# Loads that name 4 as their outermost dimension become four loads of 32 rows, and two kinds of decay rows get a DRAM array each

## The chip, the cores and the metric

The kernel runs on one core of a Trainium2 chip. Its engines are TensorE (PE, matrix products), VectorE (DVE), ScalarE (ACT), GpSimd (POOL) and SyncE (SP), which here only issues transfers; sixteen DMA engines move the data. The metric is the time of one execution on the device in microseconds (us). Three runs of the kernel before gave 586.14, 586.71 and 587.26 us; the median is 586.71.

## The reference

Three stages follow one another on 3072 tokens (4 sequences of 768). The first is a linear attention with decay, for 8 heads of width 32 and a state of 16; in chunks, with a running sum `cum` of log(a):

```
L = exp(cum_i - cum_j), zero above the diagonal
M = (C B^T) * L
y = M x + (C state) * exp(cum)
state = exp(sum log a) * state + sum_j (B_j x_j) * exp(cum_last - cum_j)
```

The second normalises each token by its root mean square and applies a gated network, `silu(xn @ w_gate) * (xn @ w_val) @ w_out`, with 256 columns in and out and 1536 between. The third is `h = x @ w_in` (1024 columns), `h * softmax(h)`, a layer norm over the 1024 columns, and a product with `w_out` back to 256 columns.

## The kernel before

The 3072 tokens are 24 units of 128 tokens; four units make a block of 512 columns, and there are six blocks. Each unit passes through the attention (functions whose names begin with `at_`), then its block through the gated network (`g_` and `o_mm`), then each unit through the third stage (`m_`). The stages of neighbouring blocks are interleaved, so that PE always has products of one block while DVE and ACT prepare another. Matrix products are made of float32 values split in a high and a low part, three products for one.

No engine chooses its work at run time. A planner (`plan`) takes a list of operations, each with an engine, an estimated duration, a due time and what it comes after, and lays them out one by one; each engine then works through its own list in that order and waits in front of an operation until its inputs are there. For SP the planner counts 8 transfers in flight at most, and its estimate of a landing goes by the `kb` and `us` of the operation. The transfers of SP carry 8 semaphores in turn (`DMAHW0` to `DMAHW7`), so a transfer is issued when the one eight before it has landed.

For one attention unit SP loads five things. `xb` (L204) is x and B of the unit, 128 rows; DVE or POOL scale its B part by the decay (L220). `cd` (L199) is C, transposed, in which the 32 rows of `bcT[u]` go to four groups of 32 partitions; it is multiplied by `e1` (L239). `L` (L216) and `e1` (L210) are decay rows: early on, `c_store` (L958) writes for each of the 192 pairs of unit and head a row of 256 numbers into the DRAM array `crow`, the first 128 for `L` and the last 128 for `e1`. `L` is that part of 8 rows given to all 128 partitions, `e1` the other part of 8 rows, each given to 16 partitions. ACT takes exponents of `L` (L226). The fifth is `bc`: B and C of the unit. For the first 12 units these are two loads of 16 rows (L194); from unit 12 (`SPLIT`) on it is one load of 512 KB that gives the 32 rows of `bcT[u]` to four groups of 32 partitions (`ld_bc4`, L308), from which B and C in high and low parts are made (L313 to L334). PE makes C B^T of a unit into the PSUM tile `pcb` (tag `hc`), DVE multiplies it with `L` (L297, L300), and the third stage's `ph` (L471) needs the same PSUM banks, so it waits for these products.

In the third stage of 20 units the 128 x 1024 block is transposed by DVE in squares of 32 (L553, into `dt`), stored to DRAM (`scr`, L559), and loaded in four pieces with the squares in their places (`tt`, four loads of 32 partitions, L566). ACT and DVE split it in high and low parts (`uth` L571, `utl` L576) for PE's product `pf` (L600). Then the result goes out (L608).

In SP's list the loads of a coming attention unit stand between the store `scr` and the reload `tt` of the unit that is in the third stage.

Of the kernel before, what the change touches and what calls it, by code (L numbers as in the profile page):

```python
# [7 lines left out]
F32 = mybir.dt.float32  # L8
# [7 lines left out]
P = 128  # L16
NU = 24
NH = 8
# [32 lines left out]
def fused_kernel(ctx, tc, aT, xbt, bcT, wg, wv, wo1, rg, wi2, wo2, gl, consts, out):  # L51
    nc = tc.nc
    V, A, G, T, S = nc.vector, nc.scalar, nc.gpsimd, nc.tensor, nc.sync
# [5 lines left out]
    dp = ctx.enter_context(tc.tile_pool(name="dram", bufs=1, space=bass.MemoryType.DRAM))  # L59
# [25 lines left out]
    la = cp.tile([P, NU * NH], F32, name="la")  # L85
    cneg = cp.tile([P, NU * NH], F32, name="cneg")
    wdec = cp.tile([P, NU * NH], F32, name="wdec")
    crow = dp.tile([NU * NH, 2 * P], F32, name="crow")


    def wt(shape, nm):
# [58 lines left out]
    wm = {}  # L150
# [45 lines left out]
    def ld_cd(u):  # L196
        d = st.setdefault(u, {})
        d["cd"] = sp.tile([P, P], F32, name="cd")
        S.dma_start(d["cd"], bcT[u][:, 512:1024].rearrange("r (q i) -> q r i", q=4))  # L199

    def ld_xb(u):
        d = st.setdefault(u, {})
# [3 lines left out]
    def ld_e1(u):  # L206
        d = st.setdefault(u, {})
        d["e1"] = sp.tile([P, P], F32, name="e1")
        r = crow[u * 8:u * 8 + 8, P:2 * P]
        S.dma_start(d["e1"], r.unsqueeze(1).to_broadcast([8, 16, P]))  # L210

    def ld_L(u):
        d = st.setdefault(u, {})
        d["L"] = sp.tile([P, 8, P], F32, name="L")
        r = crow[u * 8:u * 8 + 8, 0:P]
        S.dma_start(d["L"], r.unsqueeze(0).to_broadcast([P, 8, P]))  # L216

    def at_bw(u, e):
        bw = st[u]["xb"][:, DM:].rearrange("p (h n) -> p h n", h=8)
# [56 lines left out]
    def cbt(u):  # L276
        return u < blk[0][1] and u % 2
# [27 lines left out]
    def ld_bc4(u):  # L305
        d = st.setdefault(u, {})
        d["bc"] = sp.tile([P, 8, P], F32, name="bc")
        S.dma_start(d["bc"], bcT[u].unsqueeze(0).to_broadcast([4, 32, 1024]))  # L308

    def at_hi(u):  # L310
        d = st[u]
# [370 lines left out]
    def op(name, e, us, due, fn, after=(), new=(), use=(), lock=False, kb=0):  # L682
        ops[name] = dict(name=name, e=e, us=us, due=due, fn=fn, after=list(after), new=list(new), use=list(use),
                         lock=lock, kb=kb)

    def alt(name, us, fn):
        ops[name]["alt"] = (us, fn)
# [30 lines left out]
    for i in range(26):  # L718
        t = wdue(i)
        kind, c = pieces[i][0]  # L720
        op(f"wl{i}", "SP", 0.45, EARLY[i] if i < len(EARLY) else t - 6, (w_load, i), after=[f"wl{i-1}"] if i else [], new=[("u", f"st{i}")], kb=512)
        for k in range(3):
            op(f"wc{i}.{k}", "DVE", 0.41 if k == 0 else 0.68, t, (w_conv, i, k),
               after=[f"wl{i}" if k == 0 else f"wc{i}.{k-1}"],
               new=[("wt", f"wt{i}")] if k == 0 else [], use=[f"st{i}", f"wt{i}"], lock=True)
        if kind == "p":
            op(f"wh{i}", "ACT", 0.7, t, (p_scale, i), after=[f"wc{i}.2", "glt"] + ([f"wh{i-1}"] if c else []), use=[f"wt{i}", "w2h", "w2l"],
               new=[("uth", "w2h"), ("utl", "w2l")] if c == 0 else [])
# [18 lines left out]
    for u in range(NU):  # L747
        b, k = unit_blk[u]
        n = blk[b][1]
        if b == 0:  # L750
            Y = Y0[0] + Y0[1] * k
        else:
            Y = start[b - 1] + (k + YPOS) * (start[b] - start[b - 1]) / n * YSPAN
        s0 = u % 6 == 0
        if u >= SPLIT:
            op(f"lbc{u}", "SP", 0.45, Y - 14, (ld_bc4, u), new=[("bc", f"bc{u}")], kb=1300)
            op(f"hi{u}", "ACT", 1.15, Y - 6, (at_hi, u), after=[f"lbc{u}"] + ([f"cb{u-1}"] if u > SPLIT else []),
               new=[("wt", f"bh{u}"), ("wt", f"ch{u}")], use=[f"bc{u}", f"bh{u}", f"ch{u}"])
            op(f"bl{u}", "DVE", 0.7, Y - 5, (at_blo, u, V), after=[f"hi{u}"], use=[f"bc{u}", f"bh{u}"], lock=True)
            alt(f"bl{u}", 1.3, (at_blo, u, G))  # L760
            op(f"cl{u}", "DVE", 0.72, Y - 5, (at_clo, u), after=[f"hi{u}"], use=[f"bc{u}", f"ch{u}"], lock=True)
            op(f"c0{u}", "ACT", 0.7, Y - 4, (at_c0, u), after=[f"cl{u}"], new=[("u", f"cb{u}")], use=[f"bc{u}", f"cb{u}"])
            op(f"c1{u}", "DVE", 0.45, Y - 4, (at_c1, u), after=[f"c0{u}"], use=[f"bc{u}", f"cb{u}"], lock=True)
            cbok = [f"bl{u}", f"c0{u}", f"c1{u}"]
        else:
            op(f"lbc{u}", "SP", 0.85, Y - 9, (ld_bc, u), new=[("bc", f"bc{u}")], kb=128)
            cbok = [f"lbc{u}"]
        op(f"lxb{u}", "SP", 0.45, Y - 7.5, (ld_xb, u), new=[("xb", f"xb{u}")], kb=192)
        op(f"lcd{u}", "SP", 0.45, Y - 7, (ld_cd, u), new=[("cd", f"cd{u}")], kb=128)
        op(f"bw{u}", "DVE", 0.3, Y - 1, (at_bw, u, V), after=[f"lxb{u}", "wd"], use=[f"xb{u}"], lock=True)  # L770
        alt(f"bw{u}", 0.42, (at_bw, u, G))
        if u < NPE:
            for g in range(2):
                tg = ("pg", "pv")[g]
                op(f"lpe{u}.{g}", "PE", 0.9, Y - 5, (at_lpe, u, g), new=[(tg, f"pl{u}.{g}")], use=[f"pl{u}.{g}"],
                   after=[f"lpe{u}.{g-1}"] if g else [])
                op(f"lx{u}.{g}", "ACT", 1.3, Y - 5, (at_lpx, u, g), after=[f"lpe{u}.{g}"] + ([f"lx{u}.{g-1}"] if g else []), use=[f"pl{u}.{g}", f"L{u}"],
                   new=[("L", f"L{u}")] if g == 0 else [])
                op(f"ls{u}.{g}", "POOL", 0.57, Y - 4, (at_lselh, u, g), after=[f"lx{u}.{g}"], use=[f"L{u}"], lock=True)
            if u == 0:  # L780
                op("e1p", "PE", 0.3 * NPE, Y - 3, (at_e1pe,), new=[("po0", "pe")], use=["pe"])
                op("e1x0", "ACT", 0.6, Y - 3, (at_e1x,), after=["e1p"], new=[("th", "e1")], use=["pe", "e1"])
            e1, e1x = "e1", "e1x0"
            Lok = [[f"ls{u}.0"], [f"ls{u}.1"]]
        else:
            op(f"le1{u}", "SP", 0.45, Y - 8, (ld_e1, u), after=["crow"], new=[("e1", f"e1{u}")], kb=64)
            op(f"lL{u}", "SP", 0.6, Y - 11, (ld_L, u), after=["crow"], new=[("L", f"L{u}")], kb=512)
            op(f"lx{u}.0", "ACT", 1.3, Y - 5, (at_lexp, u, 0), after=[f"lL{u}"], use=[f"L{u}"])
            op(f"lx{u}.1", "ACT", 1.3, Y - 5, (at_lexp, u, 1), after=[f"lL{u}", f"lx{u}.0"], use=[f"L{u}"])
            op(f"ls{u}", "POOL", 1.15, Y - 4, (at_lsel, u), after=[f"lx{u}.1"], use=[f"L{u}"], lock=True)  # L790
            e1, e1x = f"e1{u}", f"e1x{u}"
            op(f"e1x{u}", "ACT", 0.3, Y - 3, (at_e1, u), after=[f"le1{u}"], use=[f"e1{u}"])
            Lok = [[f"ls{u}"], [f"ls{u}"]]
        op(f"cdm{u}", "DVE", 0.3, Y - 1, (at_cd, u, V), after=[e1x, f"lcd{u}"], use=[e1, f"cd{u}"], lock=True)
        alt(f"cdm{u}", 0.42, (at_cd, u, G))
        if u <= blk[0][1]:
            op(f"cb{u}", "PE", 1.25, Y - 2.5, (at_cb, u), after=[f"lbc{u}"] + (Lok[1] if b else []),
               new=[("hc", f"pcb{u}")] if not cbt(u) else [("t", f"pcb{u}"), ("po0", f"pcb{u}'")],
# [34 lines left out]
    for b in range(NB):  # L833
# [3 lines left out]
        for f in range(NF):  # L837
# [18 lines left out]
            for m in range(2):  # L856
                op(f"o{m}{s}", "PE", mm_us(N, 3), to, (o_mm, b, f, m), after=[f"al{s}"] + wo_n + ([f"o{m}{b}.{f-1}"] if f else []) + ([f"o0{s}"] if m else []),
                   new=[(f"po{m}", f"po{m}{b}")] if f == 0 else [], use=[f"ah{s}", f"al{s}", f"po{m}{b}"])
# [17 lines left out]
    for u in range(NU):  # L876
# [15 lines left out]
        for c in range(2) if tl else ():  # L892
            op(f"h{u}.{c}", "PE", mm_us(512, 6), H, (m_h, u, c), after=x2ok + win + ([f"h{u}.0"] if c else [f"f{min(TAIL)-1}.3"] if "t" in tags else [f"h{min(TAIL)-1}.1"]),
               new=([(tags[q], f"ph{u}.{q}") for q in range(2)] if two else [("hc", f"ph{u}")]) if c == 0 else [],
# [8 lines left out]
        for c in parts:  # L903
            op(f"ex{u}.{c}", "ACT", 0.75 if tl else 1.2, H, (m_exp, u, c), after=[f"mx{u}.2" if tl else f"mx{u}.0"] + ([f"ex{u}.0"] if c else []),
               new=[("u", f"u{u}")] if c == 0 else [], use=[hk[c], f"u{u}"])
# [18 lines left out]
        for c in range(2) if tl else ():  # L924
            if one:
                new, key = ([("hc", f"pt{u}")] if c == 0 else []), f"pt{u}"
            else:
                new, key = [(tt[c], f"pt{u}.{c}")], f"pt{u}.{c}"
# [12 lines left out]
        for c in range(4) if tl else ():  # L941
            op(f"f{u}.{c}", "PE", mm_us(DM, 6), H + 1, (m_f, u, c), after=[f"tl{u}.{c//2}"] + (wout if c == 0 else [f"f{u}.{c-1}"]),
               new=[(tt[0], f"pf{u}")] if c == 0 else [], use=[f"pf{u}"] + ku)
# [11 lines left out]
        V.tensor_copy(wm["ct"][:96, m], wm["pc", m][:96, 0:256])  # L955

    def c_store(m):
        S.dma_start(crow[96 * m:96 * m + 96, :], wm["ct"][:96, m])  # L958

    for m in range(2):  # L960
        op(f"cr{m}", "PE", 0.9, CROW, (c_rows, m), new=([("th", "ct")] if m == 0 else []) + [(("pg", "pv")[m], f"pc{m}")], use=["ct", f"pc{m}"],
           after=["cr0"] if m else [])
        op(f"cc{m}", "DVE", 0.4, CROW, (c_copy, m), after=[f"cr{m}"], use=[f"pc{m}", "ct"])
        op(f"crow" if m else "crow0", "SP", 0.45, CROW, (c_store, m), after=[f"cc{m}"] + (["crow0"] if m else []), use=["ct"], kb=96)
# [214 lines left out]
```

## Time and profile before

| | before |
|---|---|
| median of three runs | 586.71 us |
| the profiled execution | 589.83 us |
| its span | 587.9 us |
| its mean granted PE clock | 0.959 |
| PE busy | 538.1 us (92%) |
| DVE busy | 423.5 us (72%) |
| ACT busy | 310.1 us (53%) |
| POOL busy | 104.3 us (18%) |
| share of the chain that ended last: PE, DVE, DMA | 43%, 24%, 22% |
| transfers issued by SP | 282 |

The span is the time between the first and the last instruction that the profile has; the execution's own time is longer by what lies around it. The chain that ended last is followed back from the last instruction: at each step to what released it, or to the instruction before it on its engine. A wait on DMA in it lasts from the issue of a transfer to its landing, so it contains what the transfer had to wait for in the DMA engines' own queues.

### The profile page before, as it was taken

How to read it: one execution, taken by the hardware profiler on the slowest of the kernel's cores; microseconds unless marked ns; L12 is line 12 of the kernel's file. 1: busy time of each engine (PE TensorE's matmuls, PEld its weight loads, DVE VectorE, ACT ScalarE, POOL GpSimd, SP SyncE). 2: the span in 40 equal slices, each digit the busy share in tenths (PEclk: the TensorE clock that was granted, in tenths of full speed). 3: DMA queues.
4: the chain of work that ended last, by engine and by line, in shares of the span. 5: the costliest groups of instructions: out<-in, count | busy, mean ns of one | idle time of the engine just before them, and what ended most of it. 6: DMA issues, size and time to landing. Idle time of an engine off the chain costs nothing.

```text
span 587.9 us, 9064 instructions
## 1 busy us (share of the span) xinstructions
PE 538.1 (92%) x3240; PEld 447.2 (76%) x3240; DVE 423.5 (72%) x808; ACT 310.1 (53%) x670; POOL 104.3 (18%) x134
## 2 busy tenths in 40 slices
PE   8869998899999998989799888799999799998987
PEld 8758887687887876867678667588788688886886
DVE  5799999998967974767657558577675665376473
ACT  5536664666756744545645546546643434245254
POOL 2423332223211201210111102011321100010000
PEclk9679999999999999999899999989999899999789
DMA  8483774441452325426254262442420312022200
GB/s 208 123 274 114 224 223 143 157 131 67 146 188 88 125 69 158 98 78 163 69 123 112 59 171 64 116 129 55 130 82 11 107 46 80 10 71 81 80 13 34
DMA packets 59581, 64.99 MB, mean 111 GB/s; under 512 B 5200, under 2 KB 48400, under 8 KB 59536
## 3 DMA queue, kind: packets, MB, share of 16 engines
q1 hardware_dynamic: 59536, 64.41, 37.2%
q8 instruction: 25, 0.41, 0.3%
q14 instruction: 20, 0.16, 0.1%
HBM read 50.57 MB, written 13.83 MB: 110 GB/s over the span
## 4 chain that ended last, share of the span: by engine, by line
PE 43%; DVE 24%; DMA 22%; issue 4%; ACT 4%; SPq 2%; DVEq 0%; ACTq 0%
PE pf L600 11%; DMA scr<-dt 8%; DMA xb<-in_xbt_dram 8%; PE ph L471 7%; PE pg L620 7%; PE pv L620 7%; PE po L662 6%; DMA tt<-scr 4%; DVE dt L553 2%; DVE wt L117 2%; DVE th L642 2%; DVE th L638 2%; DVE utl L576 2%; DVE wt L120 2%; DVE al L654 2%
## 5 line engine op out<-in xcount | busy, mean ns | idle before, releaser
L648 ACT ACTIVATE ah<-th 128x512 fp32r<-128x512 f32 x72 | 45.2, 628 | 53.0 <-PE po L662 26.1
L226 ACT ACTIVATE L<-L,cneg 128x128 f32<-128x128 f32 x160 | 50.2, 389 | 29.5 <-DMA L<-crow 29.5
L654 DVE TENSOR_TENSOR al<-th,ah 128x512 fp32r<-128x512 f32 x65 | 46.8, 720 | 24.0 <-ACT ah L648 23.9
L620 PE MATMUL pg<-xh,wg_h 128*128 128x512 f32 x144 | 60.6, 421 | 3.4 <-DVE th L638 2.1
L600 PE MATMUL pf<-wo_h,uth 128*128 128x256 f32 x176 | 54.3, 308 | 9.5 <-ACT uth L571 9.4
L600 PE MATMUL pf<-wo_h,utl 128*128 128x256 f32 x176 | 55.5, 315 | 7.9 <-DVE utl L576 6.7
L638 DVE SCALAR_TENSOR_TENSOR th<-th,pg 128x512 f32<-128x512 f32 x72 | 49.2, 684 | 18.3 <-ACT th L634 18.2
L662 PE MATMUL po<-ah,wo_h 128*128 128x512 f32 x144 | 59.2, 411 | 0.0
L620 PE MATMUL pv<-xh,wv_h 128*128 128x512 f32 x144 | 57.9, 402 | 1.4 <-DVE th L642 1.4
L662 PE MATMUL po<-al,wo_h 128*128 128x512 f32 x144 | 56.8, 395 | 2.3 <-DVE al L654 2.3
L634 ACT ACTIVATE th<-pg 128x512 f32<-128x512 f32 x72 | 42.7, 594 | 27.9 <-PE pg L620 27.6
L620 PE MATMUL pg<-xl,wg_h 128*128 128x512 f32 x144 | 57.1, 397 | 0.0
L620 PE MATMUL pg<-xh,wg_l 128*128 128x512 f32 x144 | 57.0, 396 | 0.0
L662 PE MATMUL po<-ah,wo_l 128*128 128x512 f32 x144 | 56.7, 394 | 0.0
L620 PE MATMUL pv<-xh,wv_l 128*128 128x512 f32 x144 | 56.3, 391 | 0.0
L620 PE MATMUL pv<-xl,wv_h 128*128 128x512 f32 x144 | 56.2, 390 | 0.0
L600 PE MATMUL pf<-wo_l,uth 128*128 128x256 f32 x176 | 54.1, 307 | 0.0
L642 DVE TENSOR_TENSOR th<-pv,th 128x512 f32<-128x512 f32 x72 | 49.7, 690 | 5.7 <-PE pv L620 0.2
L471 PE MATMUL ph<-wi_h,xh 128*128 128x512 f32 x96 | 39.1, 407 | 9.5 <-DVE L L297 9.5
L600 PEld LDWEIGHTS pf<-wo_h,uth 128*128 128x128 f32 x176 | 37.6, 214 | 12.7 <-ACT uth L571 12.1
L600 PEld LDWEIGHTS pf<-wo_h,utl 128*128 128x128 f32 x176 | 38.3, 218 | 10.6 <-DVE utl L576 10.0
L536 POOL TENSOR_TENSOR sc<-sc,mhalf 128x1 f32<-128x1 f32 x24 | 13.5, 564 | 179.9 <-DVE sc L531 177.8
(150 smaller groups left out, 1219.5 us busy)
## 6 DMA issues: line engine op xcount, KB each, us to landing
L<-crow SPq DMA_DIRECT2D x20, 512.0 KB
scr<-dt SPq DMA_DIRECT2D x20, 512.0 KB
tt<-scr SPq DMA_DIRECT2D x80, 128.0 KB
bc<-in_bcT_dram SPq DMA_DIRECT2D x12, 512.0 KB
stage<-in_wo_dram SPq DMA_DIRECT2D x10, 512.0 KB
xb<-in_xbt_dram SPq DMA_DIRECT2D x24, 192.0 KB
stage<-in_wg_dram SPq DMA_DIRECT2D x6, 512.0 KB
stage<-in_wv_dram SPq DMA_DIRECT2D x6, 512.0 KB
```

Of the source, the lines that this page charges most:

```text
L117: V.scalar_tensor_tensor(out=t, in0=v[:, :, 1], scalar=-0x40000000, in1=t, op0=ALU.bitwise_and, op1=ALU.bitwise_or)
L226: A.activation(d["L"][:, h], d["L"][:, h], AF.Exp, bias=cneg[:, u * 8 + h:u * 8 + h + 1])
L471: T.matmul(ph[c], xx[:, kk, k * P:(k + 1) * P], ww[:, kk, 512 * c:512 * c + 512], start=(i == 0), stop=(i == 5))
L536: G.tensor_tensor(out=sc[:, 7:8], in0=sc[:, 6:7], in1=mhalf, op=ALU.pow)
L600: T.matmul(d["pf"][:, 0:DM], uu[:, k], ww[:, k], start=(k == 0 and i == 0), stop=(k == 7 and i == 2))
L620: T.matmul(ps[:, :n], ww[:, kk, f * P:(f + 1) * P], xx[:, kk, :n], start=(i == 0), stop=(i == 5))
L634: A.activation(d["th"], d["pg"], AF.Tanh, scale=0.5)
L638: V.scalar_tensor_tensor(out=d["th"], in0=d["th"], scalar=1.0, in1=d["pg"], op0=ALU.add, op1=ALU.mult)
L642: V.tensor_tensor(out=d["th"], in0=d["pv"], in1=d["th"], op=ALU.mult)
L648: A.activation(d["ah"], d["th"], AF.Copy)
L654: e.tensor_tensor(out=d["al"], in0=d["th"], in1=d["ah"].bitcast(F32), op=ALU.subtract)
L662: T.matmul(po[b, m][:, :n], ww[:, f, m * P:(m + 1) * P], aa, start=(f == 0 and i == 0), stop=(f == NF - 1 and i == 2))
```

## The change

The DRAM array `crow` is split by kind: `crow[0]` holds the rows for `L`, `crow[1]` those for `e1`. The 8 rows that `L` of a unit takes now lie behind one another, so its load is written with pieces of 1024 numbers (4 KB) for each partition in place of eight of 128 numbers (512 B). The store of the rows is written in two parts for each row.

Two loads whose outermost dimension was 4 (`cd` and the `bc` of the last 12 units) become four loads of 32 rows each, into the same partitions. In the planner's list their durations on SP rise from 0.45 to 1.6, and the size of the `bc` load is entered with 700 in place of 1300.

```
-    crow = dp.tile([NU * NH, 2 * P], F32, name="crow")
+    crow = dp.tile([2, NU * NH, P], F32, name="crow")
...
-        S.dma_start(d["cd"], bcT[u][:, 512:1024].rearrange("r (q i) -> q r i", q=4))
+        for q in range(4):
+            S.dma_start(d["cd"][32 * q:32 * q + 32], bcT[u][:, 512 + P * q:512 + P * q + P])
...
-        r = crow[u * 8:u * 8 + 8, P:2 * P]
+        r = crow[1, u * 8:u * 8 + 8, :]
...
-        r = crow[u * 8:u * 8 + 8, 0:P]
-        S.dma_start(d["L"], r.unsqueeze(0).to_broadcast([P, 8, P]))
+        r = crow[0, u * 8:u * 8 + 8, :].rearrange("h c -> (h c)")
+        S.dma_start(d["L"].rearrange("p h c -> p (h c)"), r.unsqueeze(0).to_broadcast([P, 8 * P]))
...
-        S.dma_start(d["bc"], bcT[u].unsqueeze(0).to_broadcast([4, 32, 1024]))
+        for q in range(4):
+            S.dma_start(d["bc"][32 * q:32 * q + 32].rearrange("p g c -> p (g c)"), bcT[u])
...
-            op(f"lbc{u}", "SP", 0.45, Y - 14, (ld_bc4, u), new=[("bc", f"bc{u}")], kb=1300)
+            op(f"lbc{u}", "SP", 1.6, Y - 14, (ld_bc4, u), new=[("bc", f"bc{u}")], kb=700)
...
-        op(f"lcd{u}", "SP", 0.45, Y - 7, (ld_cd, u), new=[("cd", f"cd{u}")], kb=128)
+        op(f"lcd{u}", "SP", 1.6, Y - 7, (ld_cd, u), new=[("cd", f"cd{u}")], kb=128)
...
-        S.dma_start(crow[96 * m:96 * m + 96, :], wm["ct"][:96, m])
+        S.dma_start(crow[:, 96 * m:96 * m + 96, :].rearrange("j r c -> r j c"),
+                    wm["ct"][:96, m].rearrange("r (j c) -> r j c", j=2))
```

The planner lays all lists out anew. The first piece of order is SP's list for one unit of the later half of the attention, with the semaphores that each transfer waits for, before (`e_...` is `e1`, `tt` the reload of `scr`):

```order
L559 DMA scr<-dt 128x1024 [waits DMAHW2_49,DVE_49]
L216 DMA L<-crow 128x8x128 [waits DMAHW3_49,PE_49]
L210 DMA e_3557<-crow 128x1x128 [waits DMAHW4_49]
L204 DMA xb<-in_xbt_dram 128x384 [waits DMAHW5_49,PE_49]
L199 DMA cd<-in_bcT_dram 128x1x128 [waits DMAHW6_49]
L566 DMA tt<-scr 32x4x256 [waits DMAHW7_49,DMAHW2_49]
L566 DMA tt<-scr 32x4x256 [waits DMAHW0_49]
L566 DMA tt<-scr 32x4x256 [waits DMAHW1_49]
L566 DMA tt<-scr 32x4x256
L308 DMA bc<-in_bcT_dram 128x1x1024 [waits DVE_49,DMAHW3_49,Activation_49,Pool_49]
L608 DMA out_dram<-ob 128x256 [waits DMAHW4_49,Activation_49]
```

The same place on SP in the changed kernel, up to the last `tt`:

```order
L561 DMA scr<-dt 128x1024 [waits DMAHW4_49,DVE_49]
L217 DMA L<-crow 128x1024 [waits DMAHW5_49,PE_49]
L211 DMA e_3647<-crow 128x1x128 [waits DMAHW6_49]
L205 DMA xb<-in_xbt_dram 128x384 [waits DMAHW7_49,PE_49]
L200 DMA cd<-in_bcT_dram 32x128 [waits DMAHW0_49]
L200 DMA cd<-in_bcT_dram 32x128 [waits DMAHW1_49]
L200 DMA cd<-in_bcT_dram 32x128 [waits DMAHW2_49]
L200 DMA cd<-in_bcT_dram 32x128 [waits DMAHW3_49]
L568 DMA tt<-scr 32x4x256 [waits DMAHW4_49]
L568 DMA tt<-scr 32x4x256 [waits DMAHW5_49]
L568 DMA tt<-scr 32x4x256 [waits DMAHW6_49]
L568 DMA tt<-scr 32x4x256 [waits DMAHW7_49]
```

The order of the kinds is the same, with `cd` as four rows (and behind it the four of `bc`, not shown). A transfer carries the semaphore that it waits for first in the row, so the four `tt` now come eight places behind `scr`, `L`, `e1` and `xb`; before, they came eight behind older transfers, and of these four the first alone waits for `scr` as well.

The second piece is DVE's list in the third stage's unit whose transposed block is stored at 340.36 us in the trace of before, from the gate's `th` up to the products with `L`, before:

```order
L638 SCALAR_TENSOR_TENSOR th<-th,pg 128x512
L409 TENSOR_SCALAR r<-y 128x1
L642 TENSOR_TENSOR th<-pv,th 128x512
L654 TENSOR_TENSOR al<-th,ah 128x512
L429 SCALAR_TENSOR_TENSOR xts<-xts,rgt,y 128x128 x2
L638 SCALAR_TENSOR_TENSOR th<-th,pg 128x512
L440 TENSOR_TENSOR xl<-xts,xh 128x2x128
L642 TENSOR_TENSOR th<-pv,th 128x512
L220 TENSOR_TENSOR xb<-xb,wdec 128x128
L297 TENSOR_TENSOR L<-pcb,L 128x512 x2
```

The same place on DVE in the changed kernel:

```order
L640 SCALAR_TENSOR_TENSOR th<-th,pg 128x512
L411 TENSOR_SCALAR r<-y 128x1
L644 TENSOR_TENSOR th<-pv,th 128x512
L656 TENSOR_TENSOR al<-th,ah 128x512
L431 SCALAR_TENSOR_TENSOR xts<-xts,rgt,y 128x128 x2
L221 TENSOR_TENSOR xb<-xb,wdec 128x128
L442 TENSOR_TENSOR xl<-xts,xh 128x2x128
L640 SCALAR_TENSOR_TENSOR th<-th,pg 128x512
L644 TENSOR_TENSOR th<-pv,th 128x512
L298 TENSOR_TENSOR L<-pcb,L 128x512 x2
```

The scaling of `xb` has moved in front of `xl` and of one pair of the gate's operations.

The third piece is SP's list at the start, behind the first weight load, before:

```order
L194 DMA bc<-in_bcT_dram 16x1024 x2
L204 DMA xb<-in_xbt_dram 128x384
L199 DMA cd<-in_bcT_dram 128x1x128
L194 DMA bc<-in_bcT_dram 16x1024 x2
L967 DMA cst<-in_consts_dram 128x264
L968 DMA rgt<-in_rg_dram 128x2x1
L204 DMA xb<-in_xbt_dram 128x384
L106 DMA stage<-in_wv_dram 128x2x512
L199 DMA cd<-in_bcT_dram 128x1x128
L971 DMA glt<-in_gl_dram 128x8x1
```

The same place on SP in the changed kernel:

```order
L194 DMA bc<-in_bcT_dram 16x1024 x2
L205 DMA xb<-in_xbt_dram 128x384
L200 DMA cd<-in_bcT_dram 32x128 x4
L194 DMA bc<-in_bcT_dram 16x1024 x2
L106 DMA stage<-in_wv_dram 128x2x512
L970 DMA cst<-in_consts_dram 128x264
L971 DMA rgt<-in_rg_dram 128x2x1
L205 DMA xb<-in_xbt_dram 128x384
L200 DMA cd<-in_bcT_dram 32x128 x4
L974 DMA glt<-in_gl_dram 128x8x1
```

The weight load of 512 KB has moved in front of the constants and of the second unit's `xb`, and each `cd` is four transfers.

## Rows read from the trace of the kernel before

**Rows 1.** Windows: stretch, its length, busy us (instructions), PE clock, DMA share, GB/s

```profile
core 0: us, PE busy (x) PEld busy (x) DVE busy (x) ACT busy (x) POOL busy (x), PEclk, DMA share, GB/s
0.00:40.00 40.00, 31.95 (x288) 28.16 (x289) 28.27 (x65) 19.49 (x54) 14.33 (x23) 0.81 0.67 188
...
135.00:225.00 90.00, 87.18 (x523) 71.81 (x521) 74.02 (x136) 55.38 (x117) 16.86 (x22) 1.00 0.39 121
225.00:410.00 185.00, 163.76 (x939) 134.67 (x937) 122.52 (x230) 99.34 (x214) 29.60 (x37) 0.96 0.39 104
...
```

**Rows 2.** Windows with one transfer in flight: `bc` (L308), `L`, `scr`

```profile
138.00:142.00 4.00, 3.77 (x17) 3.12 (x18) 3.81 (x8) 2.27 (x8) 3.67 (x5) 1.00 0.26 100
98.90:101.50 2.60, 2.60 (x22) 2.16 (x18) 2.57 (x6) 0.74 (x2) 0.00 (x0) 1.00 0.67 202
...
434.00:435.20 1.20, 1.20 (x7) 0.96 (x6) 0.73 (x4) 1.20 (x5) 0.55 (x1) 1.00 0.75 307
```

**Rows 3.** Timeline of SP's issues: start us, us of issuing, line, transfer

```profile
316.14 0.34 SPq L559 DMA_DIRECT2D scr<-dt  x1
...
337.03 0.56 SPq L308 DMA_DIRECT2D bc<-in_bcT_dram  x1
...
340.36 0.34 SPq L559 DMA_DIRECT2D scr<-dt  x1
...
342.16 3.58 SPq L204 DMA_DIRECT2D xb<-in_xbt_dram  x1
...
349.50 1.75 SPq L566 DMA_DIRECT2D tt<-scr  x4
```

**Rows 4.** Chain of waits (issue, us to landing), and SP's issue of an undisturbed `tt`

```profile
135.20 8.01 DMA bc<-in_bcT_dram
...
208.60 1.74 SPq L566 DMA_DIRECT2D tt<-scr  x4
...
209.92 2.73 DMA tt<-scr
...
342.16 10.34 DMA xb<-in_xbt_dram
```

**Rows 5.** Timeline of DVE, the same unit; in brackets the idle time and its releaser

```profile
352.52 0.29 DVE L220 TENSOR_TENSOR xb<-xb,wdec 128x128 f32<-128x128 f32 x1 [4.57 <-DMA xb<-in_xbt_dram]
352.73 1.28 DVE L297 TENSOR_TENSOR L<-pcb,L 128x512 f32<-128x512 f32 x2
```

**Rows 6.** Waits from 225 to 410 us: total us, times, longest

```profile
ACT L L226 <- DMA L<-crow: 23.7, 8, 4.2
DVE xb L220 <- DMA xb<-in_xbt_dram: 23.4, 6, 4.7
...
PE ph L471 <- DVE L L297: 9.5, 4, 2.5
```

**Rows 7.** The unit after the last `bc` load: SP's issues, chain, DVE

```profile
411.99 0.34 SPq L559 DMA_DIRECT2D scr<-dt  x1
...
415.15 1.74 SPq L566 DMA_DIRECT2D tt<-scr  x4
...
413.89 6.53 DMA xb<-in_xbt_dram
...
420.44 0.29 DVE L220 TENSOR_TENSOR xb<-xb,wdec 128x128 f32<-128x128 f32 x1 [2.42 <-DMA xb<-in_xbt_dram]
...
422.38 1.28 DVE L297 TENSOR_TENSOR L<-pcb,L 128x512 f32<-128x512 f32 x2
```

**Rows 8.** The start: two of SP's issues, then the chain of waits

```profile
0.80 0.39 SPq L1092 DMA_DIRECT2D la<-in_aT_dram  x1
...
15.13 0.47 SPq L106 DMA_DIRECT2D stage<-in_wg_dram  x1
...
8.58 4.36 DMA cd<-in_bcT_dram
...
39.10 2.96 PE pg L620 x6
```

## The prediction

> **What bounds the kernel now.** I read the page's table of slices first. TensorE (PE) is busy in most of them, so I cut the span into stretches with the view by windows and looked for the one in which PE is not busy. From 135 to 225 us PE is busy 87.18 of 90.00 us, so 3.1% is idle; from 225 to 410 us it is busy 163.76 of 185.00 us, so 21.2 us or 11.5% is idle, and its mean granted clock there is 0.96, not 1.00 [rows 1]. That stretch is where one unit (128 tokens) repeats with the same mixture of work; its period is read from two stores of the transposed block, 316.14 and 340.36: 24.2 us [rows 3]. Before 40 us PE is idle too, at a clock of 0.81, while the first loads come in [rows 8].
>
> The list of waits says what the 225 to 410 stretch waits for: VectorE (DVE) waited 23.4 us for `xb`, 6 times, ScalarE (ACT) 23.7 us for `L`, 8 times, and PE 9.5 us for DVE's product L297 [rows 6]. The product stands right behind the wait: at 352.52 DVE has sat idle for 4.57 us for `xb`, at 352.73 come the two products [rows 5], and PE's `ph` needs the PSUM banks that they free.
>
> Why is `xb` late? In SP's timeline `bc` is issued at 337.03, the store `scr` at 340.36, `xb` at 342.16 [rows 3]; the chain of waits has `xb` landing 10.34 us after that [rows 4], at 352.50. So `xb` lands 12.1 us after the store's issue. The store itself lands before the reload `tt` is issued at 349.50, so it took 9.1 us [rows 3]. Both stand behind the 512 KB `bc` load. Alone, that load takes 8.01 us [rows 4], and in a window in which nothing else is in flight the DMA share is 0.26 at 100 GB/s [rows 2]: about a quarter of the sixteen engines work, at some 385 GB/s for a full share. Whatever comes later and needs all sixteen has to wait for those four.
>
> The trace also holds the control. The unit of 411.99 us comes after the last `bc` load (twelve units have one). There `scr` has landed when `tt` is issued at 415.15, 3.2 us after its issue; `xb` lands at 413.89 + 6.53 = 420.42, 8.4 us after the store; DVE waits 2.42 us, not 4.57; the products end at 422.38 + 1.28 = 423.66, 11.7 us behind the store's issue. In the unit with a `bc` load they end at 352.73 + 1.28 = 354.01, 13.7 us behind it [rows 3, 5, 7].
>
> **The change part by part.**
>
> *The `bc` load in four (12 units).* The 512 KB go in four loads of 32 rows. The nearest rows are the four `tt` loads of 128 KB into 32 partitions: first issue 208.60, last landing 209.92 + 2.73 = 212.65, so 4.05 us for all four, against 8.01 us [rows 4]. At the longest it is 8.01 us again (no more engines used), at the shortest 512 KB at 385 GB/s, 1.4 us plus the 2.73 us of the last piece. I take 4.05. It is issued 3.3 us ahead of the store [rows 3], and so is nearly gone when the store's data move. What is gained by that is the control's difference: the products end 13.7 - 11.7 = 2.0 us earlier per unit. Units between 225 and 410 us that stand behind such a load: eight. Two things are late next. DVE's order has moved: `xb`'s scaling now stands in front of work that stood ahead of it (second piece of order), so part of the shorter wait is spent on work that was done during it. The control has that same order (its DVE does two more `th` operations and `xl` between the scaling and the products), so the 2.0 us contain that. In two of the eight units the second product has moved behind the subtraction `utl`, which needs `tt`; there I count nothing. So 6 x 2.0 = 12.0 us. Bounds: 16 us if all eight gain (and 163.76 us of PE work at the 3.1% idle of the stretch before would need 169.0, also 16.0 less than 185 [rows 1]); plus up to 6.5 us if the clock came back from 0.96 to 1.00 on 163.76 us; at the other end a loss, priced with the last rival.
>
> *`L` in 4 KB pieces.* With only `L` in flight (512 B pieces) the share is 0.67 at 202 GB/s, 301 for a full share; with only the store `scr` (4 KB pieces) 0.75 at 307, 409 [rows 2]. 512 KB then need 1.28 us, not 1.74: 0.46 us less in front of `xb`, in the six units 2.8 us. Bounds 0 to 8 x 0.46 = 3.7; nothing if the store's rate is that of writing alone. I take half, 1.4 us. The store of the rows themselves, once, now has pieces of half the size: nothing, since its 192 KB are two of 282 transfers.
>
> *`cd` in four (24 units).* It adds 72 issues; `bc`'s split adds 36. SP needs 1.75 us for four issues, 0.44 each [rows 3]; 108 are 47 us of SP, over 588 us. In the 225 to 410 stretch `cd`'s four issues (1.3 us more) lie between `xb`'s and `tt`'s, where SP now has 349.50 - 342.16 = 7.3 us for two issues [rows 3], and `tt` has to wait for the store to land anyway. Cover gone, it is 1.3 us per unit. A transfer may go when the one eight before it has landed (first piece of order): `tt`'s four now wait for `scr`, `L`, `e1` and `xb`. With `xb` at 8.4 us the fourth lands at 8.4 + 2.73 = 11.1 us behind the store; before, not earlier than 349.50 + 3 x 0.44 + 2.73 = 353.55, 13.2 us behind it. So no cost, as long as `xb` lands before 10.5 us.
>
> The Trainium skill speaks against this part. "DMA: Bandwidth & Descriptors", section "Rules for kernel authors", advises to coalesce small transfers, since under 64 KB one pays mostly overhead; a piece of `cd` has 16 KB. By that rule `cd` only loses by the split. The rows of `tt` show the four pieces overlapped (4.05 us, the last alone 2.73), so the sum by the rows stays with 1.3 us of issue under cover, and the sum by the rule would add up to 24 x 1.3 us.
>
> *The first 40 us.* SP issues there nearly back to back from 0.80 to 15.13 us [rows 8], and the chain runs through a `cd` load of 4.36 us. Four units' `cd` add 12 issues, 12 x 0.44 = 5.3 us of SP. The first gate matmul starts at 39.10 us [rows 8], behind PE and DVE work between 13 and 39 us that no load ends, so most is covered; the order of SP's loads and DVE's work there is new (third piece of order). Bounds -1 to +5.3; I take +1.5.
>
> *From 135 to 225 us* three loads are split, where PE has 2.8 us idle [rows 1]: -0.5. From 40 to 135 and behind 410 us: nothing, +-2, from the new order.
>
> Sum: -12.0 - 1.4 + 1.5 - 0.5 = -12.4. The profiled execution took 589.83 us, 1.9 more than its span of 587.9, so it would take 577.4; the median of the runs shown, 586.71, is 3.1 below the profiled execution, and 586.7 - 12.4 = 574.3. I say 574.
>
> **The rivals.**
>
> *Full recovery.* PE becomes the bound in the whole stretch: 16 us and the clock's up to 6.5, 564 to 570 with the 1.5 of the start. For it: ACT's 23.7 us of waits for `L` shrink too [rows 6], which is in my 2.0 us only as far as the control shows it. Against it: the control unit itself, with no `bc` in flight, still has DVE waiting 2.42 us. Chance 0.2, at 566.
>
> *The wait only moves.* DVE's order was made for an early `xb`; where it lands at 8.4 us and the scaling stands at about 4 us of DVE work, all that stood ahead of it is late. With 0 to 1 us per unit left: 579 to 588, at 584. For it: second piece of order. Against it: the control has that order and still gains. Chance 0.13.
>
> *The eight slots (slower).* Seventeen transfers per unit in place of eleven go through the same eight places, so `tt` is held by `xb`. If `xb` lands no earlier than now, 12.1 us behind the store, the fourth `tt` lands at 12.1 + 2.73 = 14.9 us in place of 13.2, 1.7 us later. It decides from a landing of `xb` at 10.5 us. Eight units: up to 13.6 us; PE waited for only half of such units (4 waits, [rows 6]), so 7 us: 594. It would need the four loads to use no more engines than the one did. Beside it stands the skill's rule in the same section that splitting a load into disjoint parts isn't worth it, as the parts serialize on the same sixteen engines; by that the split gains nothing. The window at a share of 0.26 speaks against it [rows 2]. Chance 0.11.
>
> **How the numbers follow.** Forecast 0.56 (568 to 581), full recovery 0.2, moved wait 0.13, slots 0.11. A measurement of this kernel tells about 0.2%, 1.2 us. Faster: 0.56 + 0.2 + 0.07 = 0.83; within 0.2%: 0.06 (of the moved wait); slower: 0.11. The range reaches from 562 to 585: it leaves out the slots and the ends of the two others.
>
> **What would show it.** In the profile after: from 225 to about 400 us PE busy 93 to 96%, its clock nearer 1.00; the period near 22.5 us; `scr` landed 3 to 5 us behind its issue; DVE's wait for `xb` under half of 23.4 us; ACT's for `L` too; no window with a share of a quarter behind a `bc` load. The first gate matmul between 38 and 44 us. I'm wrong if the store still takes 8 us or more (the split did not spread the load), if `tt`'s last load lands later than 13 us behind the store, or if the gain comes from another stretch.

## The result, and the profile after

Four runs of the changed kernel gave a median of 559.18 us (554.45 to 560.53), four of the kernel before 586.99 us (586.14 to 590.19): a ratio of 0.9502 with an interval of 0.9433 to 0.9572. The forecast was 574 us in a range of 562 to 585. The sign and the place were right, the size was less than half of what came: -27.8 us for -12.4.

The profiled execution took 554.45 us with a span of 552.6 us. It lies 4.7 us below its median, that of before (589.83 us) 2.8 us above its own, so the two traces differ by 7.6 us more than the medians do. The medians given with the experiments are over all executions, while the ratios leave out the few in the slower of the device's two states.

The windows of the changed kernel, with the columns of [rows 1]:

```profile
0.00:40.00 40.00, 32.14 (x290) 28.32 (x291) 28.18 (x66) 20.01 (x55) 13.40 (x23) 0.84 0.61 178
...
135.00:225.00 90.00, 88.55 (x533) 73.58 (x531) 76.93 (x143) 57.09 (x122) 15.88 (x20) 1.00 0.41 132
225.00:385.00 160.00, 158.92 (x975) 133.22 (x974) 124.85 (x233) 100.04 (x216) 38.41 (x40) 1.00 0.39 120
```

The stretch with the third stage's units was idle for 21.2 us of 185 on PE [rows 1]; now it is idle for 1.1 us of 160, at a granted clock of 1.00 in place of 0.96. 975 matmuls take 160 us there; before, 939 took 185. The waits of that stretch, which answer to [rows 6] (us in total, times, longest; DVE's wait in front of `utl` is a row that the prediction did not use):

```profile
ACT uth L573 <- DMA tt<-scr: 3.9, 6, 1.2
DVE xb L221 <- DMA xb<-in_xbt_dram: 2.5, 4, 0.9
ACT L L227 <- DMA L<-crow: 1.5, 2, 1.4
DVE utl L578 <- ACT uth L573: 1.0, 1, 1.0
...
PE ph L473 <- DVE L L298: 0.2, 1, 0.2
```

```profile
DVE utl L576 <- ACT uth L571: 16.4, 8, 5.4
```

The second fence is that row of before, from 225 to 410 us. One unit of the changed kernel in SP's timeline and, below it, in DVE's, answers to [rows 3, 5]:

```profile
316.77 2.69 SPq L310 DMA_DIRECT2D bc<-in_bcT_dram  x4
...
320.05 0.35 SPq L561 DMA_DIRECT2D scr<-dt  x1
...
321.75 0.43 SPq L205 DMA_DIRECT2D xb<-in_xbt_dram  x1
...
324.20 3.56 SPq L568 DMA_DIRECT2D tt<-scr  x4
```

```profile
318.77 1.25 DVE L555 STREAM_TRANSPOSE dt<-ut 128x1024 f32<-128x1024 f32 x1
...
327.44 0.29 DVE L221 TENSOR_TENSOR xb<-xb,wdec 128x128 f32<-128x128 f32 x1 [0.87 <-DMA xb<-in_xbt_dram]
330.00 1.28 DVE L298 TENSOR_TENSOR L<-pcb,L 128x512 f32<-128x512 f32 x2
331.34 1.23 DVE L578 TENSOR_TENSOR utl<-tt,uth 128x1024 fp32r<-128x1024 f32 x1
...
339.40 1.25 DVE L555 STREAM_TRANSPOSE dt<-ut 128x1024 f32<-128x1024 f32 x1
```

`tt` is issued 4.1 us behind the store (9.1 before), so the store has landed by then; `xb` lands 7.4 us behind it (12.1), the products end at 331.28, 11.2 us behind it (13.7). From one transpose to the next 20.63 us pass.

DVE's transposes (20 in each kernel, one for each unit of the third stage) date the same point of the same unit, and so tell where the time went. Start of some, and the span, in us:

| kernel | 1st | 5th | 14th | 20th | span | one unit, 5th to 14th |
|---|---|---|---|---|---|---|
| before | 149.2 | 218.7 | 431.6 | 544.9 | 587.9 | 23.7 |
| changed | 151.1 | 217.8 | 401.0 | 513.6 | 552.6 | 20.4 |
| `bc` in four alone | 150.3 | 217.7 | 398.5 | 510.6 | 551.2 | 20.1 |
| new lists alone | 154.2 | 228.9 | 450.9 | 563.4 | 603.9 | 24.7 |
| all transfers, lists of before | 148.7 | 215.7 | 395.7 | 508.1 | 547.2 | 20.0 |
| `bc` whole, behind `tt` | 152.4 | 221.7 | 403.0 | 516.4 | 559.5 | 20.1 |
| `bc` whole, ahead of `tt` | 149.7 | 235.0 | 455.7 | 568.0 | 611.1 | 24.5 |

Of the 35.3 us between the spans of before and changed, 0.9 come up to the 5th transpose, 29.7 in the nine units from there to the 14th, 0.7 up to the 20th and 4.0 behind it. The last part is one and the same work at another clock, first before, then changed:

```profile
544.90:587.90 43.00, 36.47 (x223) 33.54 (x223) 22.07 (x63) 19.54 (x41) 2.72 (x5) 0.89 0.13 43
```

```profile
513.60:552.60 39.00, 32.36 (x223) 29.53 (x223) 22.09 (x63) 19.40 (x41) 2.71 (x5) 1.00 0.15 48
```

The kernel with the new lists alone needs 40.5 us for it, so I do not credit these 4 us to the change.

### The profile page after: what moved, and what is told of

It is laid out like the page before. It is cut to its first block, busy times and chain, and to the rows that moved or that the text cites. A ratio compares the mean times of both kernels' runs of the same rounds, so it can differ in the third digit from the quotient of the medians.

```text
span 552.6 us, 9279 instructions
## 1 busy us (share of the span) xinstructions
PE 524.9 (95%) x3240; PEld 438.2 (79%) x3240; DVE 422.8 (77%) x802; ACT 309.5 (56%) x670; POOL 117.7 (21%) x140
## 4 chain that ended last, share of the span: by engine, by line
PE 64%; DVE 20%; DMA 7%; issue 4%; ACT 3%; SPq 2%; POOL 0%; DVEq 0%; ACTq 0%; POOLq 0%
PE pv L622 12%; PE pg L622 12%; PE po L664 11%; PE pf L602 11%; PE ph L473 10%; DMA xb<-in_xbt_dram 3%; DVE wt L117 3%; DVE wt L120 2%; DMA tt<-scr 2%; DVE th L644 2%; DVE th L640 2%; DVE al L656 2%; PE y L363 2%; DVE utl L578 2%; PE y L358 1%
## 5 line engine op out<-in xcount | busy, mean ns | idle before, releaser
L656 DVE TENSOR_TENSOR al<-th,ah 128x512 fp32r<-128x512 f32 x61 | 45.2, 740 | 25.7 <-ACT ah L650 25.4
L602 PE MATMUL pf<-wo_h,utl 128*128 128x256 f32 x176 | 50.8, 289 | 5.4 <-DVE utl L578 5.4
L602 PE MATMUL pf<-wo_h,uth 128*128 128x256 f32 x176 | 50.3, 286 | 4.1 <-ACT uth L573 4.1
L602 PE MATMUL pf<-wo_l,uth 128*128 128x256 f32 x176 | 50.2, 285 | 0.0
L602 PEld LDWEIGHTS pf<-wo_h,utl 128*128 128x128 f32 x176 | 34.4, 195 | 7.4 <-DVE utl L578 6.7
L602 PEld LDWEIGHTS pf<-wo_h,uth 128*128 128x128 f32 x176 | 33.9, 192 | 5.7 <-ACT uth L573 5.0
L473 PE MATMUL ph<-wi_h,xh 128*128 128x512 f32 x96 | 37.9, 395 | 0.2 <-DVE L L298 0.2
```

Source lines behind the costliest of these rows:

```text
L473: T.matmul(ph[c], xx[:, kk, k * P:(k + 1) * P], ww[:, kk, 512 * c:512 * c + 512], start=(i == 0), stop=(i == 5))
L602: T.matmul(d["pf"][:, 0:DM], uu[:, k], ww[:, k], start=(k == 0 and i == 0), stop=(k == 7 and i == 2))
L656: e.tensor_tensor(out=d["al"], in0=d["th"], in1=d["ah"].bitcast(F32), op=ALU.subtract)
```

## The experiments

**One part at a time.** First the `bc` hunk of the change alone, in the kernel before, with the lists of before.

```
-        S.dma_start(d["bc"], bcT[u].unsqueeze(0).to_broadcast([4, 32, 1024]))
+        for q in range(4):
+            S.dma_start(d["bc"][32 * q:32 * q + 32].rearrange("p g c -> p (g c)"), bcT[u])
```

> Only the bc load is split in four; lists and costs of the planner, cd and L as before. Theory 1 (the bc load held a quarter of the DMA engines, and all that came behind it waited): most of the 27.8 us comes back, 560 to 566; the store lands 3 to 5 us behind its issue, not 9.1. Theory 2 (the planner's new lists made the gain): 582 to 587. Theory 3 (L in 4 KB pieces): 582 to 587.

553.78 us (551.61 to 556.61), ratio 0.9448 [0.9383, 0.9513]: the whole gain, and more than was expected. The median lies 5.4 us below that of the whole change, though the two intervals overlap. Its window:

```profile
225.00:385.00 160.00, 159.91 (x986) 135.29 (x985) 127.02 (x242) 102.79 (x221) 31.13 (x39) 1.00 0.46 125
```

PE is idle for 0.1 us of 160. DVE no longer waits for `xb` there at all, and for `uth` in front of `utl` 2.3 us in place of 16.4. That the four loads use more of the DMA engines than the one did is seen in the unit whose loads go out from 136.74 us on:

```profile
138.00:139.50 1.50, 1.00 (x5) 0.50 (x3) 1.47 (x4) 1.32 (x3) 1.18 (x1) 1.00 0.96 268
...
141.00:143.00 2.00, 2.00 (x11) 1.62 (x10) 1.90 (x5) 0.62 (x2) 2.00 (x3) 1.00 0.00 0
```

The share is 0.96, with at most the ends of `xb` and `cd` beside the four, where it was 0.26 [rows 2], and 4.3 us after the first issue nothing is moved any more; the prediction's 4.05 us for the four fit that.

Then the rows in `crow` alone (the four hunks with `crow`):

```
-    crow = dp.tile([NU * NH, 2 * P], F32, name="crow")
+    crow = dp.tile([2, NU * NH, P], F32, name="crow")
...
-        S.dma_start(d["L"], r.unsqueeze(0).to_broadcast([P, 8, P]))
+        S.dma_start(d["L"].rearrange("p h c -> p (h c)"), r.unsqueeze(0).to_broadcast([P, 8 * P]))
```

> Only the decay rows are kept apart, so L is loaded in 4 KB pieces; bc, cd and the lists as before. Theory 1: 0.46 us less per unit of transfer time behind a bc load that still takes 8 to 11 us: 583 to 587. Theory 3: the 1024 small pieces of L fill the DMA queues and hold up the loads behind them, so most of the gain is here: 560 to 570. Theory 2: 587.

585.84 us, ratio 0.9987 [0.9951, 1.0023]. No difference that can be told; the forecast's -1.4 us is inside the interval too.

`cd` in four alone:

```
-        S.dma_start(d["cd"], bcT[u][:, 512:1024].rearrange("r (q i) -> q r i", q=4))
+        for q in range(4):
+            S.dma_start(d["cd"][32 * q:32 * q + 32], bcT[u][:, 512 + P * q:512 + P * q + P])
```

> Only the cd load is split in four, lists as before. Theory 1: cd occupied the same quarter, but for some 1 us only: 584 to 588. The eight slots in flight are dearer than thought (72 issues more, and tt behind xb): 589 to 595.

586.98 us, ratio 0.9977 [0.9926, 1.0028]: 72 issues more cost nothing that can be told, as the prediction said.

**The planner's numbers alone.** The transfers of before, laid out with the new numbers.

```
-            op(f"lbc{u}", "SP", 0.45, Y - 14, (ld_bc4, u), new=[("bc", f"bc{u}")], kb=1300)
+            op(f"lbc{u}", "SP", 1.6, Y - 14, (ld_bc4, u), new=[("bc", f"bc{u}")], kb=700)
...
-        op(f"lcd{u}", "SP", 0.45, Y - 7, (ld_cd, u), new=[("cd", f"cd{u}")], kb=128)
+        op(f"lcd{u}", "SP", 1.6, Y - 7, (ld_cd, u), new=[("cd", f"cd{u}")], kb=128)
```

> Only the planner's numbers for the two loads are changed, so all engines have the lists of the changed kernel; the transfers are those of before. Theory 2: 562 to 570. Theory 1: 585 to 593; since xb's scaling stands earlier in VectorE's list while xb lands as late as before, it may be slower than before.

606.23 us (601.54 to 609.68), ratio 1.0336 [1.0241, 1.0432]: the new lists by themselves are 19 us slower, more than was expected. One unit of it in the timelines of DVE and then of PE:

```profile
366.12 0.29 DVE L220 TENSOR_TENSOR xb<-xb,wdec 128x128 f32<-128x128 f32 x1 [5.86 <-DMA xb<-in_xbt_dram]
366.33 0.42 DVE L440 TENSOR_TENSOR xl<-xts,xh 128x256 fp32r<-128x256 f32 x1
366.74 0.69 DVE L638 SCALAR_TENSOR_TENSOR th<-th,pg 128x512 f32<-128x512 f32 x1
```

```profile
367.49 0.80 PE L620 MATMUL pg<-xh,wg_h 128*128 128x512 f32 x1 [4.61 <-DVE th L638]
```

This is the list shown in the second piece of order: `xb`'s scaling is early, DVE stands in front of it for 5.86 us (4.57 before [rows 5]), and now the gate's `th` is queued behind it, for which PE waits 4.61 us. In the changed kernel the same PE product waits 0.16 us, because `xb` is there:

```profile
329.34 0.50 PE L622 MATMUL pg<-xh,wg_h 128*128 128x512 f32 x1 [0.16 <-DVE th L640]
```

**All transfers as in the change, the planner's numbers as before** (the diff is against the changed kernel), so that the lists of PE, DVE, ACT and POOL are those of before:

```
-            op(f"lbc{u}", "SP", 1.6, Y - 14, (ld_bc4, u), new=[("bc", f"bc{u}")], kb=700)
+            op(f"lbc{u}", "SP", 0.45, Y - 14, (ld_bc4, u), new=[("bc", f"bc{u}")], kb=1300)
...
-        op(f"lcd{u}", "SP", 1.6, Y - 7, (ld_cd, u), new=[("cd", f"cd{u}")], kb=128)
+        op(f"lcd{u}", "SP", 0.45, Y - 7, (ld_cd, u), new=[("cd", f"cd{u}")], kb=128)
```

> All three transfers changed, lists of before (the planner's numbers are not changed). The bc split alone took 553.8 us with these lists, the whole change 559.2. If the new lists cost the difference: 552 to 556. If cd's 72 more issues cost it: 557 to 561.

551.78 us (548.89 to 556.0), ratio 0.9421 [0.934, 0.9502], the lowest of all that ran. PE is busy for all of the stretch:

```profile
225.00:385.00 160.00, 160.00 (x988) 135.63 (x987) 126.97 (x243) 102.87 (x222) 31.61 (x39) 1.00 0.42 126
```

Which of the two numbers costs it? The changed kernel with `cd` as before, in its load and in its number, leaves only that of `bc`:

```
-        for q in range(4):
-            S.dma_start(d["cd"][32 * q:32 * q + 32], bcT[u][:, 512 + P * q:512 + P * q + P])
+        S.dma_start(d["cd"], bcT[u][:, 512:1024].rearrange("r (q i) -> q r i", q=4))
...
-        op(f"lcd{u}", "SP", 1.6, Y - 7, (ld_cd, u), new=[("cd", f"cd{u}")], kb=128)
+        op(f"lcd{u}", "SP", 0.45, Y - 7, (ld_cd, u), new=[("cd", f"cd{u}")], kb=128)
```

> As the changed kernel, but cd stays one load with its old cost in the planner; bc (with its new cost) and L as changed. If cd's four pieces or its cost in the lists are the dear part: 552 to 556; if bc's new cost in the lists is: 558 to 561.

557.87 us, ratio 0.9496 [0.9433, 0.9558], the same as the changed kernel. So `cd`'s number is not shown to cost anything; and with the lists of before, `bc` in four and `L` in 4 KB pieces without `cd`'s split (the first two diffs of this section together):

> The kernel before with bc in four and L in 4 KB pieces, cd in one load, the lists of before. Theory 1 (cd's split is worth nothing, in four loads or in one): within 3 us of the version with all three (551.8). Rival (cd has the same fault as bc at an eighth of its size and delays what is behind it): 1 to 3 us slower than that, at bc alone, 553.8.

553.9 us, ratio 0.9437 [0.9381, 0.9492], by the ratio between the other two with the lists of before (0.9421 and 0.9448) and not told apart from either. The three versions with the lists of before have medians of 551.8 to 553.9, the two with the new lists and `bc` in four 557.9 and 559.2. Interval by interval they overlap. Taken together I put the cost of the new lists, once `xb` is early, at 4 to 7 us, an estimate from these five medians; since `cd`'s number makes no difference that can be told, it would be `bc`'s.

**How many engines.** In the changed kernel, `bc` as two loads whose outermost dimension is 2:

```
-            S.dma_start(d["bc"][32 * q:32 * q + 32].rearrange("p g c -> p (g c)"), bcT[u])
+            S.dma_start(d["bc"][64 * q:64 * q + 64], bcT[u].unsqueeze(0).to_broadcast([2, 32, 1024]))
```

> The changed kernel, with bc as two loads of 64 rows whose outermost dimension is 2. If the number of DMA engines that a load gets goes by its outermost dimension, both loads sit on two engines, bc takes 14 to 18 us and everything behind it waits longer than before the change: 600 to 640 us, DMA share about 0.13 in a window with it alone. If it is only the size of a single load that matters (theory of one big load), 256 KB pieces give a part of the gain: 560 to 580.

663.97 us (659.25 to 668.23), ratio 1.1305 [1.1215, 1.1396], slower than the 600 to 640 that were expected. A window in which the two loads alone are in flight, and the second of them in the chain of waits:

```profile
144.00:148.00 4.00, 4.00 (x19) 3.27 (x18) 0.92 (x3) 0.00 (x0) 0.09 (x1) 1.00 0.12 40
```

```profile
139.90 13.66 DMA bc<-in_bcT_dram
```

The share is half of the 0.26 in [rows 2], an eighth of the engines, for both loads together: as much as two engines, not four. So the share does go by the outermost dimension, and its price by how long what comes later stands behind.

The other way, eight loads of 16 rows:

```
-        for q in range(4):
-            S.dma_start(d["bc"][32 * q:32 * q + 32].rearrange("p g c -> p (g c)"), bcT[u])
+        for q in range(8):
+            r = 16 * (q % 2)
+            S.dma_start(d["bc"][16 * q:16 * q + 16].rearrange("p g c -> p (g c)"), bcT[u][r:r + 16])
```

> The changed kernel, with bc as eight loads of 16 rows, so 48 issues more. If the eight slots in flight and SP's issues are cheap, as the forecast had it: 557 to 562. If they are dear (a slot is held until its transfer lands, and tt comes behind bc's eight): 563 to 572.

562.33 us, ratio 0.9575 [0.9511, 0.964], some 3 us above the changed kernel, its interval overlapping. Splitting further gains nothing that can be told.

**Moved, not split.** If the gain is only that nothing stands behind the slow load, it must come without a split too, with `bc` whole at another place in SP's list; the lists of the other engines stay as before:

```
         seq = plan()
+        names = [nm for _, nm in seq]
+        for u in range(SPLIT, NU):
+            i = names.index(f"lbc{u}")
+            j = next((k for k in range(i, len(names)) if names[k][:2] == "dl"), None)
+            if j is not None and j < names.index(f"hi{u}"):
+                x = seq.pop(i)
+                seq.insert(j, x)
+                names = [nm for _, nm in seq]
```

> The kernel before with every bc load still whole (512 KB, outermost dimension 4, all sizes and pieces as before), only moved in SP's list: from behind the reload tt of one unit (where it waits for its buffer and then goes out 3 us ahead of the store) to behind the next reload tt. The lists of PE, DVE, ACT and POOL are those of before. Theory 1 (the whole gain is that scr, L, xb and tt no longer stand behind a load that occupies a quarter of the DMA engines): the load goes out where the DMA engines are idle for some 10 us, scr lands 3 to 4 us behind its issue, the period falls from 24.0 to 20 us without any split, 552 to 562 us. Theory 2 (the gain of the split is that bc itself lands earlier, or that its pieces are faster): no gain, 583 to 592.

559.1 us (556.63 to 562.24), ratio 0.9542 [0.9498, 0.9586]: 27.5 of the 34.0 us that the split alone gives, with the same load at the same quarter share. Its issues, and two windows, the first with `bc` alone in flight:

```profile
346.33 1.75 SPq L566 DMA_DIRECT2D tt<-scr  x4
348.65 0.57 SPq L308 DMA_DIRECT2D bc<-in_bcT_dram  x1
...
362.15 0.34 SPq L559 DMA_DIRECT2D scr<-dt  x1
```

```profile
352.00:356.00 4.00, 4.00 (x20) 3.29 (x19) 3.77 (x6) 4.00 (x11) 0.00 (x0) 1.00 0.25 89
...
225.00:385.00 160.00, 159.90 (x985) 134.88 (x984) 127.10 (x243) 101.98 (x220) 30.78 (x39) 1.00 0.45 128
```

The load is as slow as ever while PE is busy for all of the 4 us; it has landed before the next store (from 358 to 361 us the DMA share is 0.00). Of the 8.3 us between its span and that of the split alone, about 4 are lost up to the 5th transpose and under 0.5 in the nine units (table).

The same move with `seq.insert(j - 1, x)`: `bc` behind `xb` and `cd`, and only `tt` behind `bc`. By the prediction's own step this should have brought 12 us, since `xb` is no longer late:

> The kernel before with every bc load whole, moved in SP's list to a place between cd and the reload tt of the next unit: the store scr, L and xb are ahead of it, tt alone is behind it. This takes the wait for xb away and leaves the one behind tt (uth, then utl on DVE). By the step of the prediction (a unit is as much shorter as the products with L end earlier, 2.0 us, six to eight units): 571 to 576. Theory 1 (a unit ends behind utl, so tt's landing counts as much as xb's): xb's wait on DVE falls below 5 us in all, utl's wait for uth grows from 16.4 us, and the time is 580 to 597, no gain or a loss.

612.86 us (610.59 to 615.85), ratio 1.046 [1.0412, 1.0507], 26 us slower, and slower than even the 580 to 597 expected of the theory that `tt` counts. Of the 23.2 us between the spans, 16.3 come up to the 5th transpose and 7.8 in the nine units (table). Its waits from 225 to 410 us, and one unit of DVE with the chain's piece that ends its wait:

```profile
ACT uth L571 <- DMA tt<-scr: 41.0, 8, 6.6
DVE utl L576 <- ACT uth L571: 38.7, 8, 6.5
...
PE pf L600 <- ACT uth L571: 14.4, 8, 3.4
```

```profile
343.69 0.49 DVE L220 TENSOR_TENSOR xb<-xb,wdec 128x128 f32<-128x128 f32 x1
344.92 1.29 DVE L297 TENSOR_TENSOR L<-pcb,L 128x512 f32<-128x512 f32 x2 [0.75 <-PE pcb L341]
351.60 1.23 DVE L576 TENSOR_TENSOR utl<-tt,uth 128x1024 fp32r<-128x1024 f32 x1 [5.39 <-ACT uth L571]
...
359.15 1.25 DVE L553 STREAM_TRANSPOSE dt<-ut 128x1024 f32<-128x1024 f32 x1
```

```profile
340.92 9.49 DMA tt<-scr
```

The store goes out at 336.18 here. DVE does not wait for `xb` at all, and the products end 10.0 us behind the store, earlier than in either unit that the prediction read (13.7 and 11.7); yet `utl` starts 15.4 us behind it and the unit is as long as ever (24.25 us). The products do not end a unit.

## Why the prediction was wrong

**The step that failed** is the one that priced the split of `bc`: "the products end 13.7 - 11.7 = 2.0 us earlier per unit", counted in six of eight units, 12.0 us. Alone it measured 32 to 34 us (by the ratio, and between the medians 587.78 and 553.78). In the traces the eight units that stand behind a `bc` load took 24.0 us each before and take 20.0 with the split alone, so 4.0 less, and the ninth, the control, 20.8 and 20.7. Three things made the forecast too small.

First, the point at which I read the control. The products did come out as read (11.2 us behind the store in the changed kernel, forecast 11.7). But behind them on DVE stands `utl`, which waits for `uth` and that for `tt`, and `tt` waits for the same late store. Rows of before for the disturbed unit and for the control that I did not look at:

```profile
355.85 1.23 DVE L576 TENSOR_TENSOR utl<-tt,uth 128x1024 fp32r<-128x1024 f32 x1 [0.79 <-ACT uth L571]
...
363.00 1.25 DVE L553 STREAM_TRANSPOSE dt<-ut 128x1024 f32<-128x1024 f32 x1
...
423.58 1.22 DVE L576 TENSOR_TENSOR utl<-tt,uth 128x1024 fp32r<-128x1024 f32 x1
...
431.55 1.25 DVE L553 STREAM_TRANSPOSE dt<-ut 128x1024 f32<-128x1024 f32 x1
```

Behind their stores (340.36 and 411.99 [rows 3, 7]) `utl` starts after 15.5 and 11.6 us, the next transpose after 22.6 and 19.6. So the control's unit was not 2.0 but 3.1 us shorter. The wait that I left out is that in front of `utl`, 16.4 us in eight times (the result's second fence of waits). The last experiment shows it from the other side: `xb` early and `tt` late is no gain at all. What `xb` costs while `tt` is early, no run shows with the lists of before.

Second, two units were counted at nothing because one product had moved behind `utl`. In the changed kernel they did gain little themselves (24.0 and 24.2 us long, 1.3 and 0.1 less than before), but the unit behind each is 7.0 and 3.5 us shorter. The second of these is the control itself, so each pair gained about what its units behind a `bc` load gain elsewhere. 8 x 3.1 = 24.8 in place of 12.0 would have made the forecast 561.5. The rest, 4.0 us for 3.1, the control could not show: with the split alone the eight units are 0.7 us shorter than the control, which hardly changes, and why is open.

Third, the upper bound of 16 us, 22.5 with the clock, by which I held the full recovery for the best case. It took 163.76 us of busy PE as work and kept 3.1% idle. The same 939 matmuls at the changed kernel's 158.92 us for 975 are 153.1 us (an estimate, as the mixture may differ a little), and the split alone leaves PE idle for 0.1 us of 160. Part of the busy time was a lower clock, as the same 176 products show, before and then changed (busy us, mean ns of one):

```profile
L600 PE MATMUL pf<-wo_h,utl 128*128 128x256 f32 x176 | 55.5, 315 | 7.9 <-DVE utl L576 6.7
```

```profile
L602 PE MATMUL pf<-wo_h,utl 128*128 128x256 f32 x176 | 50.8, 289 | 5.4 <-DVE utl L578 5.4
```

From 225 to 410 us the trace of before shows where. In six of the eight units `pf`'s 24 products take 3.0 to 3.4 us at a granted clock of 1.00, as in the changed kernel (3.0). In the two others they take 5.7 and 6.5 us, most of it at 0.50, the lower of the two levels (1.2 GHz), and in both PE had just waited for `uth`, which waits for `tt`. Here is the second of them, then windows in both and in a unit at full clock:

```profile
380.15 0.58 PE L600 MATMUL pf<-wo_h,uth 128*128 128x256 f32 x1 [2.97 <-ACT uth L571]
```

```profile
285.00:287.00 2.00, 2.00 (x11) 2.00 (x11) 1.90 (x4) 1.35 (x3) 1.51 (x2) 0.50 0.00 0
357.00:359.00 2.00, 2.00 (x18) 1.88 (x17) 1.90 (x4) 0.53 (x2) 1.71 (x2) 1.00 0.00 0
382.00:385.00 3.00, 3.00 (x16) 3.00 (x16) 2.82 (x4) 2.28 (x5) 1.34 (x2) 0.50 0.00 0
```

So the clock's 6.5 us were priced about right: windows of 1 us make it some 6 us of busy time in the stretch, an estimate. The other 5 of the 10.7 us between 163.76 and 153.1 no run separates.

What came is the rival of the full recovery, which had a chance of 0.2 at 566 (564 to 570), and more than it: PE is the bound in the whole stretch. The prediction's argument against it, that the control's DVE still waits 2.42 us, took the control for a floor.

**A second error hid part of the first.** "From 40 to 135 and behind 410 us: nothing, +-2, from the new order" and the 2.0 us that were to contain the moved scaling: the new lists cost 19 us with the old transfers and 4 to 7 with the new ones. The mechanism is the one of the rival in which the wait only moves; it was real, but most of its price needs a late `xb`, which the split takes away.

**What held.** The place: 29.7 of 35.3 us lie in the nine units. The mechanism: a load on a quarter of the engines in front of four that need all. There the Trainium skill, "DMA: Bandwidth & Descriptors", "Rules for kernel authors", has the rule that an outermost dimension below 16 confines a transfer to at most as many engines; the shares of 0.26 with four and 0.12 with two agree. The Trainium skill's two rules of that section that the prediction weighed against the change did not decide here: the kernel with `bc` in four parts is 5.5% faster, as the one load's share was 0.26 and not that of sixteen engines, and `cd` in pieces of 16 KB costs nothing measurable. The forecasts for `L` (-1.4) and `cd` (0) are inside the measured intervals. The eight slots were no rival, though they are real: from 225 to 410 us SP waits in front of `tt` for `L` 4.7, for `xb` 2.8 and for `e1` 1.3 us, and for the store 6.4 us where it waited 24.0 before. The first 40 us: the gate's first product starts at 38.23 us for 39.10 [rows 8], and at 149 us the changed kernel is 1.9 us late; kernels with one and the same lists differ by as much there and more (those with the lists of before from 0.5 us early to 1.9 late, those with the new ones from 0.8 early to 5.0 late), so the +1.5 is neither shown nor refuted. Of the marks, PE's busy share (99%, not 93 to 96) and the period (20.4, not 22.5) lay beyond what I wrote, on the side of the gain.

## What to carry to other kernels

When a trace holds an undisturbed unit, compare its whole period with that of a disturbed one, from one fixed instruction to the same in the next, not the one point at which the known wait ends: another wait for the same late transfer may stand behind it. Even then the undisturbed unit need not be a floor; here the whole period gave 3.1 us a unit where 4.0 came. A ceiling on PE's gain is the number of matmuls at the rate of a stretch of the same mixture without waits, not its busy time, which a lower clock lengthens. A transfer on few engines costs by what is queued behind it: give it an outermost dimension that uses them all, or issue it where nothing follows; and look at what new durations in a planner do to the lists by themselves, since they can cost as much as the transfer gains.

## What the runs showed of the hardware

Two loads of outermost dimension 2, issued one behind the other, did not keep four engines busy: together they had a share of 0.12, and the second landed after 13.66 us, where the one load of dimension 4 took 8.01 us [rows 4]. SP's own issue of `xb` took 3.58 us behind a `bc` load [rows 3], 0.44 in the control and 0.43 in the changed kernel, so there even the issuing of what came later was held up; what holds up an issue, no run shows by itself.

PE's granted clock was 1.00 (the higher level, 2.4 GHz) for the 160 us in which it was never idle (all transfers of the change, lists of before). In the kernel before it fell to 0.50 three times from 225 to 410 us, each time after PE had waited 2.25 to 2.97 us, and the stretch's mean is 0.96 [rows 1]. In the kernel with `bc` in two, where PE is idle for 39.3 us of 160, the mean is 0.88:

```profile
225.00:385.00 160.00, 120.66 (x651) 99.45 (x649) 82.49 (x157) 66.89 (x144) 26.62 (x30) 0.88 0.28 88
```
